# Seven block products for four row tiles of dW_q, and another order of the column and m transposes, in a backward kernel on one core

## The chip, the core and the metric

The kernel runs on one core of a Trainium2 chip. The metric is the device time of one execution in microseconds (us); the time of a kernel is the median of several runs. A core has TensorE (PE: matmuls, and PEld: the loads of their stationary operand), VectorE (DVE), ScalarE (ACT), GpSimd (POOL) and SyncE (SP). Here SP does no arithmetic: it issues the transposing DMAs and some plain ones, in order. POOL issues most plain DMAs. Matmuls write to PSUM, from which VectorE and ScalarE read.

## The reference

A linear-attention block and a SwiGLU feed-forward block, each behind a layer norm with a residual, and all gradients of that. S = 2048 tokens, D = 640, 32 heads of 20, F = 1728, bf16.

```python
def _A_ref(x, wqkv, wo):
    qkv = (x @ wqkv).reshape(B, S, 3, H, Dh)...
    phi = lambda t: jnp.where(t > 0, t + 1, jnp.exp(t)) + 1e-6
    pq, pk = phi(q), phi(k)
    kv = jnp.einsum("bhsd,bhse->bhde", pk, v)
    z = jnp.einsum("bhsd->bhd", pk)
    num = jnp.einsum("bhqd,bhde->bhqe", pq, kv)
    den = jnp.einsum("bhqd,bhd->bhq", pq, z)[..., None] + 1e-6
    return (num / den)... @ wo
def _B_ref(x, w_gate, w_up, w_down):
    return (silu(x @ w_gate) * (x @ w_up)) @ w_down
h = x + _A_ref(_layernorm(x), A_wqkv, A_wo)
h2 = h + _B_ref(_layernorm(h), B_w_gate, B_w_up, B_w_down)
# outputs: h2, and the gradients to x, wqkv, wo, w_gate, w_up, w_down for a given grad_out
```

The change is about three pieces of it: the gradient dW_q = xn^T dq (640x640, a sum over 2048 tokens; xn the normalized x, dq the gradient at the query projection); the products that need transposed copies of two 640x640 matrices, GT and Y, for the gradients of wo and the value projection; and the last product of the forward pass, h2 = h + m W_down, which needs m (2048x1728) with its hidden index on the partitions.

## The kernel before

The kernel is one program of stages, each in lines below one another: the forward attention (lines 199 to 613), the gate and up projections with their gradients (622 to 897), the gradient through the feed-forward input and the second layer norm together with dp and dq (932 to 1212), and the last stage (1214 to 1599), which the change touches. Tokens are tiled in 16 tiles of 128 (ST = 16), D in 5 tiles of 128 (DT = 5), and outputs 640 wide are computed in two halves of 320 columns, so that one PSUM buffer (two banks; the pool has four buffers) holds a tile of 128x640. In a block `tc.manual_schedule(engines=...)` the named engines issue in the order of the program; the other engines are ordered by a planner that may let a later instruction go first.

The part of the program around the change, in its order:

- Lines 1170 to 1212, the end of the dp/dq stage. `dp_mm(t)` (987) makes dp of token tile t on TensorE and evicts it on ScalarE (993); `dp_1(t, ts)` (1170) does VectorE's first part (997 to 1000), widens two vectors on ScalarE (1005) and, for the tiles in `ts`, normalizes xn on ScalarE (`xn_act`, 1021); `dp_2` (1176) finishes dq on VectorE. `gt_part` (926) accumulates GT = dh1^T pqs beside it.
- Lines 1214 to 1302, a block in which SP and VectorE keep the order of the program. SP issues the 16 transposes of wqkv (1231 to 1237), the rest of GT runs on TensorE, `ps_dz` follows (1257 to 1262), and `load_pk` (1222), `load_pqT` (1275), `wk2` (1279) and `dwqk_steps` (1285) are defined. `dwqk(0, i)` is row tile i of dW_q: 2 halves x 16 token tiles = 32 matmuls of 128x320, an eviction on ScalarE (1295) and a store from POOL (1296).
- Lines 1304 to 1322: `dwqk(0, 0)`, the masked blocks `kv_blocks` (534, 540 and 543) that need all of GT, `dwqk(0, 1)`, `wk2(0..4)` mixed with `dwqk(0, 2)`, and the broadcast `ps_dzb`. Each `wk2(i)` is 7 small matmuls, an eviction and a transpose on SP (1283).
- Lines 1338 to 1390, the dk loop, with steps t = 0 to 18. Step t makes dk of token tile t (10 matmuls at 1353, VectorE at 1350, 1354 and 1356, a transpose on SP at 1357), and, for token tile u = t - 3, dxn (30 matmuls at 1382, three products of which the last needs the transposed dk) and the layer norm's backward pass (`ln_bwd`, 143). SP also issues two transposes for tile u + 3 in each step (`load_pqT`). Steps 2 and 3 begin with `dwqk(0, 3)` and `dwqk(0, 4)`. Steps 8 to 13 transpose the six column blocks of GT (`tr_cols`, 1361). Step 14 transposes KV. Step 16 loads w_down (1369, 1371). From u = 11 on (`MTA = 5`) each step transposes one m tile (`load_mT`, 1330), which is 128 tokens x 1792. From step 16 on, `dwqk(1, i)` does row tiles of dW_k.
- Lines 1509 to 1599, the last part, with TensorE, ScalarE and POOL in the order of the program. It computes m W_down for two token tiles at a time by seven block products (`step_a` to `step_f`, p = 0 to 6; `osum` makes the block sums of m on VectorE, 1430) and the last two tiles directly (`tail`, 1571). Before it SP transposes m tiles 5 and 6 and Y columns 0 and 1, then in step p = 0, 1, ... m tiles 2p+7 and 2p+8 and Y columns 2p+2 and 2p+3. Small products (`dwo`, `dwv`) go between the steps from a queue, `small_q`; the last two `dwv` stand after the first half of tile 14 and before `step_d(6)`.

The m tiles live in four tiles of a pool with four buffers that also holds dq, the transposed ring and wvk; so each group of four m tiles can only be loaded when one of these has been read for the last time. `mats` is one 17x640 region of SBUF in which GT, woT, dKVT, KV, G, Y and a sum in fp32 follow one another.

Of the kernel before, what the change touches and what calls it, by code (L numbers as in the profile page):

```python
# [8 lines left out]
FP32 = mybir.dt.float32  # L9
# [6 lines left out]
P = 128  # L16
# [4 lines left out]
def kernel(  # L21
# [23 lines left out]
    GM = 448  # L45
    MTA = 5
    HKG = 13
# [884 lines left out]
    with tc.manual_schedule(engines={EngineType.PE, EngineType.DVE, EngineType.Activation, EngineType.SP, EngineType.Pool}):  # L932
# [237 lines left out]
        def dp_1(t, ts=()):  # L1170
            dp_a(t, prs[t % 2])
            widen(rxs[t % 2], rall, t)
            xn_act(ts)
            widen(prs[t % 2], nS1, t)
# [5 lines left out]

        dp_1(ST - 5)
        dp_mm(ST - 4)
        dp_1(ST - 4)
        dp_2(ST - 5)
# [3 lines left out]
        dp_mm(ST - 3)  # L1188
        dp_1(ST - 3, range(6, 8))
        dp_2(ST - 4)  # L1190
# [22 lines left out]

    with tc.manual_schedule(engines={EngineType.SP, EngineType.DVE}):

# [6 lines left out]
        def load_pk(t):  # L1222
            pkrs[t] = small.tile([P, D], BF16, name="pkr", tag="stg", bufs=3, padded_shape=[P, 7 * P])
            pool_store(pkrs[t][:], scr_pk_v[:, t, :])

        load_pk(0)
        load_pk(1)
        def tr_cols(dst, src, c):
            nc.sync.dma_start_transpose(out=dst.unsqueeze(1), in_=src[:, c:c + P])
# [80 lines left out]
        nc.vector.tensor_tensor(out=half(zacc), in0=row(ps_dz), in1=half(dmask[:]), op=ALU.mult)  # L1310
        dwqk(0, 0)
        kv_blocks(dKVT, "ps_dkvt", lambda i, a, b: woT[:, i, a:b], lambda i, a, b: GT[:, i, a:b])
        dzs = [wk("dzs"), wk("dzl")]
        nc.vector.tensor_copy(out=dzs[0][:], in_=zacc)
        nc.vector.tensor_tensor(out=dzs[1][:], in0=zacc, in1=dzs[0][:], op=ALU.subtract)
        dwqk(0, 1)
        for i in range(3):
            wk2(i)
        dwqk(0, 2, lambda: [wk2(i) for i in range(3, DT)])
        ps = mm("ps_dzb")  # L1320
        mm_row(ps, lambda k: ones[:], lambda k, n0, n1: dzs[k][:, n0:n1], 2)
        nc.scalar.copy(out=half(dzb[:]), in_=row(ps))

        dk = big.tile([P, ST, D], BF16, name="dk", tag="B")
        mTs = {}
# [12 lines left out]
        for t in range(ST + LAG):  # L1338
            if t >= ST:
                for i in ((0,), (1, 2), (3,))[t - ST]:  # L1340
                    load_h1(i)
            if t in (2, 3):
                dwqk(0, t + 1)
            if t < ST:
                if t + 2 < ST:
                    load_pk(t + 2)
                if t in (2, 6):
# [8 lines left out]
                nc.vector.tensor_tensor(out=dk[:, t, :], in0=tk[:], in1=pkr[:], op=ALU.mult)  # L1356
                nc.sync.dma_start_transpose(out=ring[:, t % 4], in_=dk[:, t, :])
                if t < 2:
                    load_pqT(t + 1)
            if 8 <= t < 8 + HG:  # L1360
                tr_cols(G[:, t - 8, :], scr_GT, OH[t - 8])
            if t == 14:
# [21 lines left out]
            if u + 3 < ST:  # L1384
                load_pqT(u + 3)
            if ST - MTA <= u:
                load_mT(u - ST + MTA)
            dx = wk("dx")
# [120 lines left out]
        with tc.manual_schedule(engines={EngineType.PE, EngineType.Activation, EngineType.Pool}):  # L1509
            for t in (4, 5):  # L1510
                load_h1(t)
            for t in (5, 6):
                load_mT(t)
            for j in range(2):
                tr_cols(Y[:, j, :], scr_Yt, OH[j])
            tt(T1, B12, B11)
# [14 lines left out]
            for p in range(NP):  # L1531
                v = p - 1
                for t in (2 * p + 4, 2 * p + 5):
                    if p > 0 and t < ST:
                        load_h1(t)
                for t in (2 * p + 7, 2 * p + 8):
                    if t < ST:
                        load_mT(t)
                for j in range(2 * p + 2, min(2 * p + 4, HG)):
                    tr_cols(Y[:, j, :], scr_Yt, OH[j])  # L1540
                step_a(p)
# [36 lines left out]
            tail(ST - 2, 0, 320, p14[:, 0, :320])  # L1578
            for f, i in small_q:
                f(i)  # L1580
            step_d(v)
            tail(ST - 2, 320, D, p14[:, 1, :320])
            c22(v)
# [46 lines left out]
```

## Time and profile before

| | us |
|---|---|
| median of 3 runs | 791.06 (788.67 to 811.74) |
| the profiled execution's own time | 790.5 |
| its span, first to last instruction | 788.8 |
| mean granted TensorE clock | 0.996 of full speed |

Read the profile so: the busy time of an engine is the sum of its instructions; TensorE's matmuls are pipelined, so the duration of one (about 299 ns for 128x320) is longer than the distance between two starts. "Waits" give, for an engine and a line, how long the engine stood idle before it, and which instruction released it. The chain of waits is followed back from the last instruction. The DMA share is the mean busy share of 16 DMA engines; packets that wait in a queue count, so it can be above 1. The stages in time: the dp/dq stage ends near 586, dW_q and wk2 run from 586 to 617 with the first four dk tiles, the dk loop from 617 to 711, and the last product from 711 to 786.

### The profile page before, as it was taken

Reading aid. Unit: us, or ns where it says so; the run is one execution under the profiler, and the core shown is the slowest. Engines: PE = TensorE matmul, PEld = TensorE weight load, DVE = VectorE, ACT = ScalarE, POOL = GpSimd, SP = SyncE. Lnnn points to the kernel's source line nnn. Section 1 sums busy time; section 2 is a strip of 40 time slices with the busy share of each in tenths; the row PEclk is TensorE's granted clock in tenths of the full one; section 3 lists DMA queues with packets and bytes.
Section 4 is the critical chain, followed back from the end, with each engine's and each line's share of the span. In section 5 each row is a group of like instructions: output and inputs, shape, how many; then the busy total and the mean of one; then the engine's idle time right before and its main releaser. Section 6 shows DMA issues by size and latency. Waiting matters only on the chain.

```text
span 788.8 us, 13752 instructions
## 1 busy us (share of the span) xinstructions
PE 778.6 (99%) x5243; PEld 500.3 (63%) x5243; DVE 575.9 (73%) x1005; ACT 331.6 (42%) x490; POOL 224.8 (28%) x380
## 2 busy tenths in 40 slices
PE   9999999999999999999999999999999999999988
PEld 7676566555555555555666677777767777777756
DVE  7979988894788548848888668999862466627753
ACT  6962532670184036501841245667652233323001
POOL 4600037513301120145231444341421122123310
PEclk9999999999999999999999999999999999999989
DMA  9799999999979997999899899999899888999992
GB/s 263 162 243 307 200 220 280 264 246 227 227 178 224 203 214 179 238 256 225 208 230 161 282 268 187 211 241 221 182 249 176 160 187 174 170 253 222 211 222 77
DMA packets 295012, 170.54 MB, mean 216 GB/s; under 512 B 242765, under 2 KB 282702, under 8 KB 294945
## 3 DMA queue, kind: packets, MB, share of 16 engines
q1 hardware_dynamic: 271472, 102.75, 66.0%
q0 software_dynamic: 20032, 63.34, 29.0%
q10 hardware_dynamic: 3440, 3.56, 1.4%
q8 instruction: 41, 0.67, 0.4%
q14 instruction: 27, 0.21, 0.1%
HBM read 52.84 MB, written 56.28 MB: 138 GB/s over the span
## 4 chain that ended last, share of the span: by engine, by line
PE 91%; DVE 3%; DMA 2%; SPq 2%; issue 1%; ACT 1%; POOL 0%; ACTq 0%; DVEq 0%
PE ps_dw L881 10%; PE ps_dxn L1382 8%; PE ps_wa L690 7%; PE pg L796 7%; PE pu L801 7%; PE ps_dhn L955 7%; PE ps_dwqk L1290 6%; PE ps_dm L423 5%; PE ps_dhc L955 5%; PE ps_kq L311 4%; PE ps_wc L690 3%; PE ps_dk L110 3%; PE ps_y L514 3%; PE ps_a L577 3%; PE ps_oa L1446 2%; PE pdm L423 2%
## 5 line engine op out<-in xcount | busy, mean ns | idle before, releaser
L955 PEld LDWEIGHTS <-cols 128*128 128x128 bf16 x624 | 61.0, 98 | 23.8
L796 PE MATMUL pg<-wgu,hnT 128*128 128x448 bf16 (+1 forms) x320 | 63.6, 346 | 0.0
L801 PE MATMUL pu<-wgu,hnT 128*128 128x448 bf16 (+1 forms) x320 | 63.6, 346 | 0.0
L881 PE MATMUL ps_dw<-m_s,dh 128*128 128x448 bf16 (+1 forms) x320 | 60.4, 346 | 0.0
L1382 PEld LDWEIGHTS <-ring 128*128 128x128 bf16 x480 | 47.0, 98 | 18.2
L1382 PE MATMUL ps_dxn<-wqkvT,ring 128*128 128x320 bf16 x320 | 51.3, 299 | 0.0
L801 PEld LDWEIGHTS <-hnT 128*128 128x128 bf16 x320 | 31.3, 98 | 27.1
L881 PEld LDWEIGHTS <-dh 128*128 128x128 bf16 x320 | 31.3, 98 | 27.1
L796 PEld LDWEIGHTS <-hnT 128*128 128x128 bf16 x320 | 31.3, 98 | 27.0
L423 PEld LDWEIGHTS <-dh2T 128*128 128x128 bf16 x320 | 31.0, 98 | 25.1
L423 PE MATMUL ps_dm<-wdT,dh2T 128*128 128x448 bf16 (+1 forms) x240 | 46.5, 344 | 0.0
L817 ACT ACTIVATE dd<-pg 128x896 bf16<-128x896 f32 (+1 forms) x32 | 28.5, 890 | 40.4 <-PE pg L796 40.4
L311 PE MATMUL ps_kq<-wqk,xnT 128*128 128x320 bf16 x320 | 44.9, 299 | 0.6 <-DMA xnT<-xn 0.5
L311 PEld LDWEIGHTS <-xnT 128*128 128x128 bf16 x320 | 30.8, 98 | 13.0 <-DMA xnT<-xn 0.9
L690 PEld LDWEIGHTS <-S 128*128 128x128 bf16 x256 | 25.0, 98 | 21.7
L1290 PEld LDWEIGHTS <-hn 128*128 128x128 bf16 x320 | 31.0, 98 | 12.1 <-issue 0.3
L140 POOL TENSOR_SCALAR lnv<-mv 128x1 f32<-128x1 f32 x32 | 11.9, 373 | 89.8 <-DVE mv L136 73.8
L843 POOL DMA_DIRECT2D scr_m<-m_s x16 | 12.1, 757 | 88.0 <-DVE m_s L829 88.0
L148 DVE CUSTOM_DVE_ANT_0 lb_a<-lb_dy,hn 128x640 bf16<-128x640 bf16 x16 | 13.2, 826 | 30.2 <-ACT lb_dy L146 29.3
L686 DVE TENSOR_TENSOR dd<-dd 128x3584 bf16<-128x3584 bf16 (+1 forms) x12 | 23.1, 1954 | 13.4 <-PE ps_wa L690 13.4
L146 ACT ACTIVATE lb_dy<-ps_dxn,rstd 128x640 bf16<-128x640 f32 x16 | 12.7, 793 | 45.1 <-PE ps_dxn L1382 45.1
L977 POOL DMA_DIRECT2D dh<-lb_a x16 | 14.6, 910 | 58.1 <-DVE lb_a L976 57.7
(261 smaller groups left out, 1797.5 us busy)
## 6 DMA issues: line engine op xcount, KB each, us to landing
scr_dT<-stg SPq DMA_DIRECT2D x48, 224.0 KB, 3.2
cols<-scr_dT POOLq DMA_DIRECT2D x21, 448.0 KB, 6.1
scr_m<-m_s POOLq DMA_DIRECT2D x12, 448.0 KB, 4.8
pq<-scr_pq POOLq DMA_DIRECT2D x32, 160.0 KB, 5.8
hn<-in_A_x_dram SPq DMA_DIRECT2D x5, 640.0 KB, 5.7
scr_dT<-stg SPq DMA_DIRECT2D x16, 192.0 KB, 2.3
cols<-scr_dT POOLq DMA_DIRECT2D x7, 384.0 KB, 5.6
scr_pq<-pqa SPq DMA_DIRECT2D x4, 640.0 KB, 4.5
```

The lines of the kernel that those rows point to most:

```text
L110: nc.tensor.matmul(ps[:, ci, :320], lhsT=lhs(k), rhs=rhs(k, *NCH[ci]), start=(start and k == 0), stop=(stop and k == n - 1))
L311: nc.tensor.matmul(ps[:, ci, :320], lhsT=xnT[:, t, k, :], rhs=wqk[:, k, w0 + n0:w0 + n1], start=(k == 0), stop=(k == DT - 1))
L423: nc.tensor.matmul(ps[:, c, :w], lhsT=dh2T[:, kt, (t + c) * P:(t + c + 1) * P], rhs=wdT[:, kt, o:o + w], start=(kt == 0), stop=(kt == DT - 1))
L514: nc.tensor.matmul(ps[:, ci, :320], lhsT=xn[:, t, i * P:(i + 1) * P], rhs=pk[:, t, n0:n1], start=(t == 0), stop=(t == ST - 1))
L690: nc.tensor.matmul(out, lhsT=lhs[:, t, :], rhs=rhs[:, t, :], start=(first and t == 0), stop=(t == 7), skip_group_check=not first)
L796: nc.tensor.matmul(pg[:, c, :w], lhsT=hnT[:, kt, (t + c) * P:(t + c + 1) * P], rhs=wg[:, kt, 0:w], start=(kt == 0), stop=(kt == DT - 1))
L801: nc.tensor.matmul(pu[:, c, :w], lhsT=hnT[:, kt, (t + c) * P:(t + c + 1) * P], rhs=wg[:, kt, w:2 * w], start=(kt == 0), stop=(kt == DT - 1))
L817: sig = nc.scalar.activation(out=dg, in_=pg[:, :, :w], func=ACT.Sigmoid)
L881: nc.tensor.matmul(ps[:, c, :w], lhsT=lhs(t), rhs=rhs(t), start=(t == 0), stop=(t == ST - 1))
L955: nc.tensor.matmul(out, lhsT=lhs[:, k, :], rhs=rhs[:, k, :], start=(first and k == 0), stop=(k == HKG - 1), skip_group_check=not first)
L1290: nc.tensor.matmul(ps[:, ci, :320], lhsT=xn_r[:, t, i * P:(i + 1) * P], rhs=dq[t // 8][:, t % 8, n0:n1] if which == 0 else dk[:, t, n0:n1] ...
L1382: nc.tensor.matmul(ps[:, ci, :320], lhsT=lhs[:, i, :], rhs=rhs[:, i, n0:n1], start=(k == 0 and i == 0), stop=(k == 2 and i == DT - 1))
```

## The change

Four parts, all in the last two stages:

1. Row tiles 0 to 3 of dW_q are computed as a 2x2 block problem: rows in two halves of two row tiles each (m = 0, 1, with u = 0, 1 inside), tokens in two halves of 8 tiles (k = 0, 1), columns in two halves of 320 (n = 0, 1). Seven products of 8 matmuls for each u replace eight. The sums of blocks that they need (T of dq, 8x320 per partition; S of xn, 8x128) are made on VectorE, and so are the combinations; ScalarE copies partial results from PSUM to SBUF. Three of the four PSUM buffers are held by the products meanwhile. Row tile 4 keeps its 32 matmuls and stands in the middle, and the `wk2` are between the products. The last product of u = 0 and 1 (`p3q`) is done in steps 0 and 1 of the dk loop, and its combinations (`c12q`) in step 1. `kv_blocks` moves ahead of all of them. TensorE and ScalarE now keep the order of the program in this block and so through the dk loop.
2. GT's columns are transposed in steps 3 to 8 of the dk loop, Y's in steps 8 to 13; the third pkr tile is loaded ahead, and the others by the end of a step instead of the beginning of the next.
3. The m tiles start at u = 10: tile 0 to 2 in u = 10 to 12, two each in 13 and 14, one in 15 (`MT_AT`). The last part then transposes m tiles 2p+8 and 2p+9 in step p, with no Y columns between.
4. Two passes of `xn_act` move to the two `dp_1` before, one each, and the last `dwv` moves behind `step_d(6)`.

```diff
@@ -43,7 +43,7 @@
     NKT = 27
     FT = 14
     GM = 448
-    MTA = 5
+    MT_AT = (10, 11, 12, 13, 13, 14, 14, 15)
     HKG = 13
     assert (S, D, F) == (2048, 640, 1728)
 
@@ -1178,15 +1178,15 @@
             load_q(t + 3)
             return last
 
-        dp_1(ST - 5)
+        dp_1(ST - 5, range(6, 7))
         dp_mm(ST - 4)
-        dp_1(ST - 4)
+        dp_1(ST - 4, range(7, 8))
         dp_2(ST - 5)
         for i in (0, 1):
             gts[i] = mm("ps_gt")
             gt_part(gts[i], i, 0, ST - 4, ST if i else 4)
         dp_mm(ST - 3)
-        dp_1(ST - 3, range(6, 8))
+        dp_1(ST - 3)
         dp_2(ST - 4)
         nc.gpsimd.dma_start(out=hn[:, ST - 4:ST, :], in_=x_v[:, ST - 4:ST, :])
         store_dwd(p - 1)
@@ -1211,7 +1211,7 @@
         xn_act(range(9, ST - 4))
         last_dq = dp_2(ST - 1)
 
-    with tc.manual_schedule(engines={EngineType.SP, EngineType.DVE}):
+    with tc.manual_schedule(engines={EngineType.SP, EngineType.DVE, EngineType.PE, EngineType.Activation}):
 
         wqkvT = big.tile([P, 16, D], BF16, name="wqkvT", tag="B")
         xn_r = hn
@@ -1225,6 +1225,7 @@
 
         load_pk(0)
         load_pk(1)
+        load_pk(2)
         def tr_cols(dst, src, c):
             nc.sync.dma_start_transpose(out=dst.unsqueeze(1), in_=src[:, c:c + P])
 
@@ -1308,20 +1309,98 @@
                                         scalar2=rstd1[:, t:t + 1], op0=ALU.subtract, op1=ALU.mult)
         zacc = mats[:, 15 * D:17 * D].bitcast(FP32)
         nc.vector.tensor_tensor(out=half(zacc), in0=row(ps_dz), in1=half(dmask[:]), op=ALU.mult)
-        dwqk(0, 0)
         kv_blocks(dKVT, "ps_dkvt", lambda i, a, b: woT[:, i, a:b], lambda i, a, b: GT[:, i, a:b])
+
+        dk = big.tile([P, ST, D], BF16, name="dk", tag="B")
+        dkf = dk.rearrange("p t d -> p (t d)")
+        U2 = (0, 1)
+        NB = 8 * 320
+        Ta = dkf[:, 16 * D - NB - 16 * P:16 * D - 16 * P].rearrange("p (k n) -> p k n", k=8)
+        S3q = [dkf[:, 16 * D - 8 * P * (2 - u):16 * D - 8 * P * (1 - u)].rearrange("p (k c) -> p k c", c=P) for u in U2]
+        Tb = mat(2 * HG * P, 8, 320)
+        Sq = [mat(2 * HG * P + NB + 8 * P * u, 8, P) for u in U2]
+
+        def xb(m, k, u):
+            return xn_r[:, 8 * k:8 * k + 8, (2 * m + u) * P:(2 * m + u + 1) * P]
+
+        def db(k, n):
+            return dq[k][:, :, 320 * n:320 * n + 320]
+
+        def vv(out, in0, in1, op=ALU.subtract):
+            nc.vector.tensor_tensor(out=out, in0=in0, in1=in1, op=op)
+
+        def kept():
+            return wk("kept", pool=1)[:].bitcast(FP32)
+
+        def prod8(out, lhs, rhs, start=True):
+            for k in range(8):
+                nc.tensor.matmul(out, lhsT=lhs[:, k, :], rhs=rhs[:, k, :], start=(start and k == 0), stop=(k == 7),
+                                 skip_group_check=not start)
+
+        pq_a = [mm("ps_dwa") for _ in U2]
+        Aq = [p[:, 0, :320] for p in pq_a]
+        Dq = [p[:, 1, :320] for p in pq_a]
+        for u in U2:
+            prod8(Aq[u], xb(0, 0, u), db(0, 0))
+        s1q = [kept() for _ in U2]
+        for u in U2:
+            nc.scalar.copy(out=s1q[u], in_=Aq[u])
+        vv(Ta, db(0, 1), db(0, 0))
+        for u in U2:
+            prod8(Dq[u], xb(0, 1, u), db(1, 0))
+            vv(Sq[u], xb(1, 0, u), xb(1, 1, u), ALU.add)
+        pq_c = mm("ps_dwc")
+        for u in U2:
+            prod8(pq_c[:, u, :320], Sq[u], Ta)
         dzs = [wk("dzs"), wk("dzl")]
         nc.vector.tensor_copy(out=dzs[0][:], in_=zacc)
         nc.vector.tensor_tensor(out=dzs[1][:], in0=zacc, in1=dzs[0][:], op=ALU.subtract)
-        dwqk(0, 1)
-        for i in range(3):
-            wk2(i)
-        dwqk(0, 2, lambda: [wk2(i) for i in range(3, DT)])
+        ev0, ev1 = ([wk("dwq") for _ in U2] for _ in U2)
+        for u in U2:
+            vv(ev0[u][:, 0:320], Dq[u], s1q[u], ALU.add)
+        dwqk(0, 4)
+        vv(Tb, db(1, 1), Ta)
+        for u in U2:
+            vv(Sq[u], Sq[u], xb(0, 0, u))
+        for u in U2:
+            vv(S3q[u], xb(0, 0, u), xb(1, 0, u))
+        vv(Ta, db(1, 1), db(0, 1))
+        u2q = [kept() for _ in U2]
+        for u in U2:
+            prod8(Aq[u], Sq[u], Tb, False)
+            nc.scalar.copy(out=u2q[u], in_=Aq[u])
+            wk2(u)
+        vv(Tb, db(1, 0), Tb)
+        for u in U2:
+            vv(Sq[u], xb(0, 1, u), Sq[u])
+        for u in U2:
+            prod8(Aq[u], S3q[u], Ta, False)
+            nc.scalar.copy(out=s1q[u], in_=Aq[u])
+            wk2(2 + u)
+        for u in U2:
+            vv(ev1[u][:, 320:D], pq_c[:, u, :320], s1q[u], ALU.add)
+
+        def dwq_store(i, ev):
+            nc.gpsimd.dma_start(out=out_2[i * P:(i + 1) * P, 0:D], in_=ev[:])
+
+        for u in U2:
+            prod8(Aq[u], xb(1, 1, u), Tb, False)
+            nc.scalar.copy(out=ev1[u][:, 0:320], in_=Aq[u])
+            dwq_store(2 + u, ev1[u])
+            if u == 0:
+                wk2(4)
         ps = mm("ps_dzb")
         mm_row(ps, lambda k: ones[:], lambda k, n0, n1: dzs[k][:, n0:n1], 2)
         nc.scalar.copy(out=half(dzb[:]), in_=row(ps))
 
-        dk = big.tile([P, ST, D], BF16, name="dk", tag="B")
+        def p3q(u):
+            prod8(pq_c[:, u, :320], Sq[u], db(1, 1), False)
+
+        def c12q():
+            for u in U2:
+                vv(ev0[u][:, 320:D], pq_c[:, u, :320], u2q[u], ALU.add)
+                dwq_store(u, ev0[u])
+
         mTs = {}
 
         def load_mT(t):
@@ -1339,11 +1418,9 @@
             if t >= ST:
                 for i in ((0,), (1, 2), (3,))[t - ST]:
                     load_h1(i)
-            if t in (2, 3):
-                dwqk(0, t + 1)
+            if t < 2:
+                p3q(t)
             if t < ST:
-                if t + 2 < ST:
-                    load_pk(t + 2)
                 if t in (2, 6):
                     load_xnT(2 + t // 6)
                 pkr = pkrs.pop(t)
@@ -1355,10 +1432,16 @@
                                                in1=half(dzb[:]), op0=ALU.mult, op1=ALU.add)
                 nc.vector.tensor_tensor(out=dk[:, t, :], in0=tk[:], in1=pkr[:], op=ALU.mult)
                 nc.sync.dma_start_transpose(out=ring[:, t % 4], in_=dk[:, t, :])
+                if t + 3 < ST:
+                    load_pk(t + 3)
+                if t == 1:
+                    c12q()
                 if t < 2:
                     load_pqT(t + 1)
+            if 3 <= t < 3 + HG:
+                tr_cols(G[:, t - 3, :], scr_GT, OH[t - 3])
             if 8 <= t < 8 + HG:
-                tr_cols(G[:, t - 8, :], scr_GT, OH[t - 8])
+                tr_cols(Y[:, t - 8, :], scr_Yt, OH[t - 8])
             if t == 14:
                 nc.sync.dma_start_transpose(out=KV.rearrange("p j c -> p (j c)").unsqueeze(1), in_=scr_KVT)
             if t == ST:
@@ -1383,8 +1466,8 @@
                                          start=(k == 0 and i == 0), stop=(k == 2 and i == DT - 1))
             if u + 3 < ST:
                 load_pqT(u + 3)
-            if ST - MTA <= u:
-                load_mT(u - ST + MTA)
+            for i in [i for i, v in enumerate(MT_AT) if v == u]:
+                load_mT(i)
             dx = wk("dx")
             ln_bwd(ps, xn_r[:, u, :], rstd1[:, u:u + 1], dh1[:, u, :], dx[:], 0)
             nc.gpsimd.dma_start(out=o1_v[:, u, :], in_=dx[:])
@@ -1509,10 +1592,6 @@
         with tc.manual_schedule(engines={EngineType.PE, EngineType.Activation, EngineType.Pool}):
             for t in (4, 5):
                 load_h1(t)
-            for t in (5, 6):
-                load_mT(t)
-            for j in range(2):
-                tr_cols(Y[:, j, :], scr_Yt, OH[j])
             tt(T1, B12, B11)
             osum(0, 0)
             tt(T2, B22, T1)
@@ -1533,11 +1612,9 @@
                 for t in (2 * p + 4, 2 * p + 5):
                     if p > 0 and t < ST:
                         load_h1(t)
-                for t in (2 * p + 7, 2 * p + 8):
+                for t in (2 * p + 8, 2 * p + 9):
                     if t < ST:
                         load_mT(t)
-                for j in range(2 * p + 2, min(2 * p + 4, HG)):
-                    tr_cols(Y[:, j, :], scr_Yt, OH[j])
                 step_a(p)
                 if v < 0:
                     tt(T4, B21, T2)
@@ -1576,9 +1653,10 @@
             v = NP - 1
             p14 = mm("ps_o")
             tail(ST - 2, 0, 320, p14[:, 0, :320])
-            for f, i in small_q:
-                f(i)
+            (f, i), (f2, i2) = small_q
+            f(i)
             step_d(v)
+            f2(i2)
             tail(ST - 2, 320, D, p14[:, 1, :320])
             c22(v)
             step_e(v)
```

## The prediction

> **What bounds the kernel now.** I read the page's busy times first, then the waits of TensorE alone, then the chain that ended last from 740 us on, then the busy time by stretches. TensorE is the bound:
>
> ```profile
> span 788.8 us, 13752 instructions
> ...
> PE 778.6 (99%) x5243; PEld 500.3 (63%) x5243; DVE 575.9 (73%) x1005; ACT 331.6 (42%) x490; POOL 224.8 (28%) x380
> ```
>
> It is idle for 10.2 us in all, so an edit can win only by giving it fewer instructions, or by ending a wait of TensorE itself. These three of its waits lie where the change works (us in total, times, longest):
>
> ```profile
> PE ps_oa L1446 <- DVE h1r L1430: 3.5, 1, 3.5
> ...
> PE ps_dp L110 <- ACT dp L993: 0.8, 1, 0.8
> PE ps_dwv L129 <- ACT dwv L1405: 0.8, 1, 0.8
> ```
>
> The chain (start, duration, what) tells what is behind the 3.5 us: not VectorE, but an m tile, and before it the Y columns on SP's queue.
>
> ```profile
> 740.09 1.34 SPq L1229
> 741.43 0.04 issue
> 741.48 2.58 SPq L1229
> 744.05 0.04 issue
> 744.09 10.85 DMA mT<-scr_m
> 754.95 0.02 issue
> 754.97 0.96 DVE os L1430 x2
> 755.93 0.41 DVE h1r L1430
> 756.34 0.04 issue
> 756.38 3.36 PE ps_oa L1446 x12
> ```
>
> In program order the transposes at L1330 give that m tile as number 11. VectorE had finished at 750.09 and stood until it came. The stretches (length, then PE, PEld, DVE, ACT, POOL busy, granted clock, DMA share, GB/s) show what it cost and where room is:
>
> ```profile
> 617.00:686.00 69.00, 69.00 (x510) 49.70 (x509) 42.33 (x98) 21.65 (x36) 14.07 (x27) 1.00 0.85 168
> ...
> 711.00:752.84 41.84, 41.84 (x313) 30.18 (x312) 29.85 (x58) 6.96 (x11) 13.50 (x25) 1.00 1.18 225
> 752.84:756.38 3.54, 0.00 (x1) 0.00 (x0) 1.41 (x4) 0.69 (x1) 0.00 (x0) 0.80 1.27 218
> 756.38:759.00 2.62, 2.62 (x10) 1.43 (x10) 1.84 (x4) 0.00 (x0) 1.62 (x3) 0.50 0.94 173
> 759.00:762.00 3.00, 3.00 (x14) 1.72 (x13) 0.98 (x2) 0.00 (x0) 0.54 (x1) 0.54 1.18 240
> ```
>
> After the idle 3.54 us the granted clock is 0.50 and 0.54 until 762. From 617 to 686 TensorE never stops and the DMA engines have room; after 711 they have none.
>
> **The change part by part.** Times are on the clock of the profile before; the sum is made against its own 790.5 us (span 788.8 and 1.7 around it). The median of the runs shown, 791.06, is 0.6 above that.
>
> *Products.* Four row tiles go from 4x32 matmuls of 320 columns to 7x2x8 = 112. The chain gives the price:
>
> ```profile
> 592.09 4.35 PE ps_dwqk L1290 x32
> ```
>
> That is 0.136 us each, so 16 fewer save 2.18 us. What pays for it on VectorE:
>
> ```profile
> L686 DVE TENSOR_TENSOR dd<-dd 128x3584 bf16<-128x3584 bf16 x9 | 17.9, 2021 | 11.2 <-PE ps_wa L690 11.2
> ...
> L686 DVE TENSOR_TENSOR S<-hn 128x1024 bf16<-128x1024 bf16 x16 | 10.1, 685 | 8.2 <-DMA stg<-dd 6.6 <-DMA out_dram<-dwd 1.6
> ...
> L1430 DVE TENSOR_TENSOR ot<-ps_oa,h1r 128x320 f32<-128x320 f32 x14 | 6.9, 492 | 10.2 <-PE ps_oa L1446 5.0 <-PE ps_oa L1452 4.8
> ```
>
> Eight sums of 1024 at 0.69 are 5.5 us, four of 2560 at 1.49 (between the two rows: (2021-685)/2560 = 0.522 ns an element) are 5.9, six combinations of 320 at 0.49 are 2.9: 14.3 us, where VectorE was busy 8.3 us of the 31 between 586 and 617. ScalarE loses four evictions of 0.69 and gets eight of 320 columns at about 0.53 (the 128x320 rows of L1038), 1.5 us more.
>
> Do they come in time? The key blocks now follow ps_dz at once (586.1); the last GT copy ended at 585.73, so ps_dz covers it. VectorE is done with zacc and the four masks near 588.5, with Ta at 590.0, with the two Sq at 591.3. TensorE spends 587.6 to 592.0 on four products, then wants Sq and Ta: 1.4 us (first Sq) in hand. The kept row tile (4.35 us) covers the casts, the two combinations, Tb, Sq, S3q and the second Ta, which end at 595.1, 596.5, 597.9 and 599.4; they are wanted at 598.5, 598.5, 601.4 and 601.4. The third Tb can start when its readers end at 601.2, ends at 602.7 and is wanted at 604.3. So about 1.5 us is in hand everywhere. On ScalarE each step asks 0.53+0.69 = 1.2 us against 0.35+1.09 = 1.4 us on TensorE (7 matmuls of wk2, 8 of the product); the one bank pair left for wk2 is given back just in time. In a fixed order a late item stalls all behind it: everything up to the dk tiles queues behind such a product, and dxn behind those. The nearest case is the same scheme in the gate and up gradients (L690), where the waits of TensorE list nothing: 0. From the other side, all the hands-over late by 0.1 us and one sum late by its own 1.5 us: 2.5. I take 0, as the L690 case is nearest.
>
> *Start of the dk loop.* The two row tiles that stood between the dk tiles (8.7 us) now stand ahead, so dk 0 has less time. From the start of its matmuls to its transpose on SP took 3.07 us (602.70 to 605.77). Now: start 608.6, issue 611.7, landing 3.6 later (median of ring<-dk; 2.6 to 6.1 seen): 615.3. TensorE is there after dk 0, the late product, dk 1 to 3 (5x1.36 less 0.27) and ten matmuls of dxn 0 (1.36), at 616.5: 1.2 us in hand; a landing of 6.1 costs 1.3 us. I take 0, the median; range 0 to 1.3.
>
> *SP's queue, 617 to 686.* The columns of GT move from steps 8-13 to 3-8, those of Y from the last stage to 8-13. Y's six transposes are new there. GT's took 1.22 to 1.41 us of SP each, and in their steps TensorE kept its 5.43 us: a step with four transposes asks about 5.1 us of SP. SP starts step 3 some 3 us late (backlog of the pq and pk transposes), gains 0.4 us a step, loses 0.9 at step 8, which has five. Behind these wait the pq tiles, issued within 5 us of the dxn that frees their slot and wanted 12.2 us after it: with 4 us of landing the hand is 3 to 4 us less the backlog, never below 0 by much. At nothing; without that cover see the slower rival.
>
> *The m tiles.* They begin at row 10: eight instead of five are issued inside the loop, at 3.5 us of SP each for the first, and delay dk 15, pq 14, pq 15 and the wd load by some 3 us. Of these the nearest is wd: landed at 710.5, wanted at 715.45, so 2 us stay. From about 711.5 SP then stands at m tile 4, as before (711.4), and goes straight on: the six Y transposes between (718.46-721.95, 732.04-735.17, 740.09-744.05) took 10.6 us. So m tile 11 is issued near 733.5 instead of 744.1 and with 10.85 us to land is there near 744.4; it was wanted at 750.1. The wait goes: 3.54 us, and the slow clock behind it: 22 matmuls from 756.38 to 762.00 took 5.62 us, at 0.136 they take 2.99, so 2.63. Together 6.17. Late next would be m tile 13: two tiles at 3.5 us behind, near 751 to 752, wanted near 757. Bounds: 0 if it lands as late as before, 6.17 if not; I take 6.17, by 5.7 us in hand.
>
> *A rule against this row.* The Trainium skill, "TensorE: Matmul & The Clock Gate", Part 1, has the clock fall to half after an idle window of about 3.4 us and come back after about 3.4 us of work. By that the slow stretch would cost an estimated 1.7 us and not 2.63, and the sum would be 9.1. The row, 0.50 to 0.54 for 5.6 us, decides.
>
> *A rule against the move.* The skill's "Trainium Kernel Development and Optimization", Key Constraints, says that transfers of all queues run on the same 16 DMA engines; so moving Y takes no DMA work away. By that alone the tail would keep its wait and the sum would be 3.8. The stretches (0.85 before 686, 1.18 after 711) show that it goes where room is.
>
> *Small waits.* Two ScalarE passes over hn (1.73 us at 569.64) stood ahead of the eviction that TensorE waited for; one each now goes into earlier idle gaps of ScalarE of 1.93 and 1.77 us. Saves 0.83. The last dwv goes behind six products and two matmuls (1.09 us) that cover the eviction of 0.69: saves 0.82. Both between 0 and that. POOL's pkr loads move by part of a step, with three buffers as before; the two xnT loads behind the third pkr come 2 us later, landed by 592 for 608: nothing.
>
> Sum: 2.18 + 6.17 + 0.83 + 0.82 = 10.0. 790.5 - 10.0 = **780.5 us**.
>
> **The rivals.**
> *The m tiles stay late.* Between 720 and 730, and 741 and 750, single m tiles held SP for 6.8 and 6.1 us; if copies slow the transposes wherever they stand, tile 11 or 13 is late again. Against it: 5.7 us in hand. All of the 6.17 lost: 786.7; a part, with a wait too short for the slow clock: about 783.
> *The block or dk 0 waits.* For it: hands of 1.2 to 1.5 us and a fixed order. 2.5 + 1.3 = 3.8 lost: 784.3.
> *SP's queue becomes the bound from step 3 to 13 (slower).* 45 transposes in 11 steps of 5.43 us (59.7). At 1.27 each they take 57; at 1.72 (the two Y transposes at 718.46, 3.44 us, beside other traffic) 77.4, which is 13 us over after the hand of 4.5: 793.7. It decides from (59.7+4.5+10)/45 = 1.65 us each. Against it: GT's 1.22 to 1.41 in this very loop.
>
> **How the numbers follow.** Forecast 0.70, m tiles late 0.13, block or dk 0 late 0.09, SP's queue 0.06, and 0.02 for a gain beyond it. The low end is the forecast less 1.8, by which the fastest run shown (788.67) lies under the profiled one: 778.7. The high end, 788.0, holds the first two rivals and 1.3 more; the third is outside. Two per cent, about what a measurement of this kernel can tell from no change, is 15.8 us: below 775 there is no term (0.03), above 807 only SP's queue at more than 2 us a transpose (half of its 0.06, so 0.03), within 0.94.
>
> **What would show it.** Right: 16 matmuls fewer, and among TensorE's waits no ps_oa, ps_dp or ps_dwv; clock 1.00 through 762; steps of 5.43 us in the dk loop. Wrong: a TensorE wait on VectorE or on an eviction between 586 and 610; a first dxn that waits for ring; steps longer than 5.43 us with SP never waiting for dk; the chain again ending in mT<-scr_m.

## The result, and the profile after

The changed kernel takes 790.70 us (median of 20 runs, 787.10 to 805.34), the kernel before on the same chip 786.78 us (20 runs, 783.88 to 811.74). The ratio, from the undisturbed runs of both, is 1.0059, 95% interval 1.0036 to 1.0081: some 4.6 us slower. The forecast was 780.5 us, and its range ended at 788.0.

The profiled executions alone would mislead: 789.3 us after, 790.5 us before. The one of before lies 3.7 us above the median of its 20 runs, and it carried the wait in the last stage and the slow clock in full. More on that below.

The busy times of the page after (span 787.6 us):

```profile
PE 776.4 (99%) x5227; PEld 498.3 (63%) x5227; DVE 589.1 (75%) x1023; ACT 332.4 (42%) x494; POOL 224.9 (29%) x380
```

TensorE has the 16 matmuls fewer that were foretold. Its waits in the same execution (us in total, times, longest):

```profile
PE ps_dxn L1465 <- DMA ring<-dq: 5.6, 1, 5.6
...
PE ps_dxn L1465 <- DMA ring<-dk: 1.1, 1, 1.1
```

All three waits that the change aimed at are gone (ps_oa, ps_dp, ps_dwv). Two new ones stand in the dk loop: dxn waits for a ring tile, once dk, once dq. By stretches (length, then PE, PEld, DVE, ACT, POOL busy, granted clock, DMA share, GB/s):

```profile
614.00:648.70 34.70, 27.93 (x203) 19.31 (x201) 20.28 (x46) 9.02 (x15) 8.93 (x16) 0.99 1.10 192
648.70:655.70 7.00, 7.00 (x42) 4.54 (x43) 0.33 (x1) 0.88 (x2) 0.00 (x0) 0.79 1.05 185
...
717.00:758.00 41.00, 41.00 (x304) 29.52 (x303) 31.13 (x61) 6.96 (x11) 13.49 (x25) 1.00 1.21 209
```

The block of products (586 to 607) has no gap, nor has the last stage (the third line) up to 758, at clock 1.00. What is lost lies between 614 and 656: 34.70 - 27.93 = 6.77 us idle, then a slow clock. The chain of what ended last (start, duration, what) leads back from the first wait to VectorE, from the second to SP's queue:

```profile
614.07 0.60 DVE tk L1431
614.67 7.50 DMA ring<-dk
...
637.51 2.05 SPq L1277
...
639.61 9.04 DMA ring<-dq
...
648.70 5.65 PE ps_dxn L1465 x30
...
655.71 4.07 PE ps_dxn L1465 x30
```

The first late tile is dk 1. SP issued it as soon as VectorE had made it; what is long is its landing, 7.50 us. The second is the dq of tile 5. It stood behind other transposes in SP's queue, was issued in step 5 at 639.61, only 3.5 us before dxn wanted it (643.15; before, 634.68 and 644.00: 9.3 us ahead), and landed 9.04 us later. The 30 matmuls behind it take 5.65 us, and 4.07 a step later: 1.58 us of slow clock. Waits and clock together cost 1.12 + 5.55 + 1.58 = 8.25 us. This nearly closes the account of the two profiled executions: products -2.21, last stage -3.54 and -2.63, small waits -0.83 and -0.82 are -10.03; with the 8.25 that is -1.8, and the spans differ by -1.2.

SP's own queue after (start, duration, what it issues):

```profile
610.70 1.20 SPq L1434 DMA_TRANSPOSE ring<-dk  x1
...
614.67 1.21 SPq L1434 DMA_TRANSPOSE ring<-dk  x1
...
619.63 5.78 SPq L1434 DMA_TRANSPOSE ring<-dk  x2
...
629.47 1.22 SPq L1434 DMA_TRANSPOSE ring<-dk  x1
...
634.75 1.22 SPq L1434 DMA_TRANSPOSE ring<-dk  x1
```

and before:

```profile
605.77 1.20 SPq L1357 DMA_TRANSPOSE ring<-dk  x1
...
609.72 1.22 SPq L1357 DMA_TRANSPOSE ring<-dk  x1
...
629.24 1.27 SPq L1277 DMA_TRANSPOSE ring<-dq  x1
632.11 1.20 SPq L1357 DMA_TRANSPOSE ring<-dk  x1
...
634.68 1.27 SPq L1277 DMA_TRANSPOSE ring<-dq  x1
```

Two differences are to be seen. First, dk 0 and dk 1 were issued at 605.77 and 609.72 and would have been wanted near 618.2 and 623.6: 12.4 and 13.9 us. Now they are issued at 610.70 and 614.67 and wanted near 615.5 and 620.9: 4.8 and 6.3 us. Second, a step had three transposes (dk, pk, dq), and after the dq SP had nothing to issue for 1.6 us (630.51 to 632.11); now it has four, and from dk to dk 629.47 to 634.75 is 5.28 us of a step of 5.43. In both kernels a few transposes hold SP longer than the usual 1.2 to 1.3 us, up to 2.87 in this profile of before and up to 4.00 after; the pair at 619.63 is one of 4.00 and one of 1.69.

So the theory to be tested was: two losses that add. (1) With the products ahead, the 8.7 us of two dW_q row tiles no longer stand between the dk tiles, and a tile of the first steps that comes late stops TensorE. (2) With four transposes a step in steps 3 to 13, SP cannot work off a hold, and dq or dk comes late at a later step. The rivals: the 640 KB xnT load of step 6 as such; POOL's burst of loads and stores at the loop's start; the order of the pk and pq transposes.

### The profile page after: what moved, and what is told of

The parts are those of the page before. It is cut to its first block, busy times and chain, and to the rows that moved or that the text cites. A ratio compares the mean times of both kernels' runs of the same rounds, so it can differ in the third digit from the quotient of the medians.

```text
span 787.6 us, 13759 instructions
## 1 busy us (share of the span) xinstructions
PE 776.4 (99%) x5227; PEld 498.3 (63%) x5227; DVE 589.1 (75%) x1023; ACT 332.4 (42%) x494; POOL 224.9 (29%) x380
## 4 chain that ended last, share of the span: by engine, by line
PE 91%; DVE 3%; DMA 3%; issue 1%; SPq 1%; ACT 0%; POOL 0%; DVEq 0%; ACTq 0%
PE ps_dw L881 10%; PE pu L801 7%; PE ps_wa L690 7%; PE pg L796 7%; PE ps_dxn L1465 7%; PE ps_dhn L955 7%; PE ps_dm L423 5%; PE ps_dhc L955 5%; PE ps_kq L311 4%; PE ps_oa L1529 4%; PE ps_dwqk L1291 3%; PE ps_wc L690 3%; PE ps_y L514 3%; PE ps_a L577 3%; PE pdm L423 2%; PE ps_dp L110 2%
## 5 line engine op out<-in xcount | busy, mean ns | idle before, releaser
L955 PE MATMUL ps_dhn<-wgT,cols 128*128 128x320 bf16 x208 | 30.8, 299 | 0.0
```

The source lines that it names most:

```text
L955: nc.tensor.matmul(out, lhsT=lhs[:, k, :], rhs=rhs[:, k, :], start=(first and k == 0), stop=(k == HKG - 1), skip_group_check=not first)
```

## The experiments

"Waits" below are those of TensorE from 586 us on in the kernel's profiled execution, in us at their time.

**Undoing the transposes, and making the moves alone.** e1 puts GT's columns back to steps 8 to 13 and Y's back to the last stage; the m tiles stay as changed:

```diff
-            if 3 <= t < 3 + HG:
-                tr_cols(G[:, t - 3, :], scr_GT, OH[t - 3])
             if 8 <= t < 8 + HG:
-                tr_cols(Y[:, t - 8, :], scr_Yt, OH[t - 8])
+                tr_cols(G[:, t - 8, :], scr_GT, OH[t - 8])
...
+                for j in range(2 * p + 2, min(2 * p + 4, HG)):
+                    tr_cols(Y[:, j, :], scr_Yt, OH[j])
```

> The changed kernel with the columns of GT back in steps 8 to 13 and those of Y back in the last stage; products and m tiles as changed. Theory: the wait of dxn for ring<-dq (5.6 us and some 1.6 us of slow clock in the profile after) needs GT's columns in steps 3 to 8, which keep SP's backlog alive until the 640 KB xnT load of step 6. Then the dk loop has no wait over 1.5 us here, and the time is about 3.8 us under the kernel before (16 matmuls, 0.83, 0.82), ratio 0.995. Rival, the products alone: with the 8.7 us of TensorE work moved ahead of the dk loop the wait stays, ratio 1.005.

Measured: 789.21 us, ratio to before 0.9991 (0.9951 to 1.0032). Waits: dq 1.75 at 622.4, dk 4.66 at 628.6, Y for ps_dwv 2.7 in two. The late dq of steps 5 and after is gone, the waits of the first steps are there: loss (1) stands without loss (2). Y in the last stage behind the new m tiles makes a wait of its own. The profiled execution took 795.71 us, 6.5 us above the median of e1, so these sizes are not those of a usual run.

e2 is the kernel before with the moves of G, Y and the m tiles alone; its edit is the lines of the diff on `MT_AT`, `tr_cols` and `load_mT`.

> The kernel before with the moves of GT, Y and the m tiles alone; dW_q, the order of TensorE and the small waits as before. Theory: without the late start of the dk loop SP has no backlog at step 3, so no wait in the dk loop, and no wait for an m tile in the last stage; ratio 0.993 to 0.998, by how large that wait is in the usual run of the kernel before. Rival, the moves alone: TensorE waits for ring<-dq or ring<-pk in the dk loop, 5 us or more, ratio 1.005 or above.

Measured: 786.82 us, ratio 0.9976 (0.9946 to 1.0005). No wait for an m tile; dq 1.59 at 679.3, and the two small waits of before (0.83, 0.82). So the moves gain some 0.24% (1.9 us, and the interval reaches just over 1), not the 6.17 us of the forecast, and bring a late dq near the end of the loop.

**The 640 KB load.** e3 cuts the two xnT loads of steps 2 and 6 into eight of 160 KB:

```diff
+        def load_xnT1(v):
+            pool_store(xnT_r[:, v], scr_xnT[v])
...
-                if t in (2, 6):
-                    load_xnT(2 + t // 6)
+                if 2 <= t < 10:
+                    load_xnT1(t + 6)
```

> The changed kernel with the two 640 KB loads of xnT at steps 2 and 6 cut into eight of 160 KB, one in each of steps 2 to 9. Theory: the large load is what holds SP's transposes for about 4 us at step 6 and makes dq 5 late; in pieces the dk loop's waits fall from 6.7 us to under 2, and the time is 5 to 7 us under that of the changed kernel, ratio 0.992 to 0.998 to the kernel before. Rival: the 160 KB of each step and four transposes are too much together in any form; the waits stay and the ratio stays near 1.006.

Measured: 789.92 us, ratio 1.0034 (1.0003 to 1.0065). Waits on dq of 0.90 at 627.8, 3.08 at 636.5, 0.58 and 0.21. Cutting the load up does not remove the waits, it moves them. What the place of the load does is seen in e9, below.

**Before, once more.** e4 is the kernel before, for a second profile.

> The kernel before unchanged, for a second profile of it. Theory: the wait for m tile 11 that the forecast took away whole (3.54 us and 2.63 us of slow clock) is larger in the first profile (790.5 us) than in the usual run (median 786.8); here the time is 784 to 787 and that wait is under 2 us with no slow clock behind. Rival: the wait is as large in each run, and something else makes the usual run faster.

Measured: 791.33 us. Its longest TensorE wait:

```profile
PE ps_oa L1446 <- DVE h1r L1430: 4.9, 3, 4.1
```

The wait in the last stage is real and comes back (4.08 at the longest), but both profiled executions lie well above the median: of 116 runs of before in these comparisons 80 had a mean granted clock of 1.000, these two 0.996 and 0.998.

This profile shows something else, which the first profile of before does not. Here is its dk 1, the 640 KB load that POOL issues beside it, and, in the view of that one transpose, its landing:

```profile
611.86 1.31 SPq L1357 DMA_TRANSPOSE ring<-dk  x1
...
611.94 0.76 POOL L165 DMA_DIRECT2D xnT_r<-scr_xnT  x1
```

```profile
DMA to landing us min/median/max: 10.0/10.0/10.0
```

So dk 1 lands as late as in any changed kernel (9.99 us, at 621.85), and another dk holds SP for 5.27 us, yet the dk loop has no wait: dk 1 was wanted at 623.54, 11.7 us after its issue. With 7.6 us less lead it would have been late by 5.9 us.

**The products alone.** e5 is the changed kernel with G, Y and the m tiles in the places of before.

> The changed kernel with the columns of GT and Y and the m tiles all as before; products, fixed order, small waits and the early third pkr tile as changed. Theory: the products alone already cost most of what they save, since SP starts the dk loop late: a dxn of tile 1 to 6 waits 2 us or more for ring<-dq or ring<-dk, the fastest run is near 783 (3 us over the 780.3 that the fastest run before less 3.8 gives), ratio 0.997 to 1.002. Rival: the products cost nothing and only GT's early columns do; then no such wait, ratio 0.995 or less.

Measured: 788.94 us, ratio 1.0017 (0.9985 to 1.0049). One long wait, the transpose that it waited for, and SP behind it:

```profile
PE ps_dxn L1463 <- DMA ring<-dk: 4.0, 1, 4.0
```

```profile
617.51 10.40 DMA ring<-dk
```

```profile
623.20 7.54 SPq L1434 DMA_TRANSPOSE ring<-dk  x2
```

The late tile is dk 1 again. It was issued 3.97 us behind dk 0, as in the kernel before (3.95), and took 10.40 us to land. The next two, dk 2 and dk 3, hold SP for 4.73 and 2.71 us (7.54 with the 0.10 between), but come in time. That is loss (1) by itself: the products, which save 2.2 us of TensorE, save nothing.

**Order on SP and POOL.** Three tries to give the first dk tiles a freer queue. e6 issues pqT(1) before the loop and pqT(2) in step 0; e7 issues the third pkr load behind the two xnT loads instead of ahead; e8 does both.

```diff
 e6
+        load_pqT(1)
         ps = mm("ps_dzb")
...
-                if t < 2:
-                    load_pqT(t + 1)
+                if t == 0:
+                    load_pqT(2)
 e7
-        load_pk(2)
...
         load_xnT(0)
         load_xnT(1)
+        load_pk(2)
```

> The changed kernel with the pq and pk transposes of tile 1 issued before the dk loop, where SP stood idle for 2.6 us (608.1 to 610.7 in the profile after), and those of tile 2 in step 0. Theory: the waits come from SP's backlog at the start of the loop, which is 2.5 to 5 us smaller now and can't be worked off later at 5.28 us of SP in a step of 5.43: the waits of dxn fall from 6.7 us to under 3, the time by 3 to 6 us, ratio 0.997 to 1.001. Rival: the four transposes in each of steps 3 to 13 are too much wherever the loop starts; the waits only come later, ratio 1.004 or above.

> The changed kernel with the third pkr load behind the first two xnT loads on POOL's queue, so that these go 2.5 us earlier, as before. Theory: they then collide less with SP's transposes of wqkv, which end at 595 to 597 in place of 598.6, and SP's backlog is some 2 us smaller: ratio 1.001 to 1.004. Rival: the end of the wqkv transposes is set by the 800 KB store of GT, which does not move: end at 598 to 600 and ratio 1.006 as the changed kernel.

> The two edits together (pq and pk transposes of tile 1 ahead of the dk loop, third pkr load behind the xnT loads). Theory: backlog 4 to 6 us smaller, no wait of dxn over 1.5 us, ratio 0.993 to 0.998. Rival: as in the two before, ratio 1.004 or above.

Measured: e6 794.08 us, ratio 1.0058 (1.0014 to 1.0101), dk 2.09 at 624.8 and dq 0.35; e7 791.74 us, 1.0041 (1.0001 to 1.0082), dq and dk late five times, up to 2.97; e8 791.44 us, 1.0063 (1.0025 to 1.0102), dk 4.18 and dq 1.59. None helps, though e8's wqkvT transposes ended at 595.0 (598.5 in the changed kernel). The order of these few transfers is not the cause. In all three the late dk is dk 1. The profiled execution of e6 took 784.96 us, 9 us under its median, so its two waits do not explain that median.

**Burst apart, cover back.** e9 moves, in the program, two of POOL's stores from step 1 to steps 3 and 4 and the xnT loads from steps 2 and 6 to 5 and 9. e10 gives part of the cover back: one row tile (4.35 us) goes from the middle of the products to step 2 of the dk loop. e11 does both, and e12 does both with G, Y and the m tiles in the places of before.

```diff
 e9
-                dwq_store(u, ev0[u])
...
-                if t in (2, 6):
-                    load_xnT(2 + t // 6)
+                if t in (3, 4):
+                    dwq_store(t - 3, ev0[t - 3])
+                if t in (5, 9):
+                    load_xnT(2 + t // 9)
 e10
-        dwqk(0, 4)
         vv(Tb, db(1, 1), Ta)
...
             if t < 2:
                 p3q(t)
+            if t == 2:
+                dwqk(0, 4)
```

> The changed kernel with the copies that POOL issues at steps 1 to 3 spread: the two last dW_q stores at steps 3 and 4, the xnT loads at steps 5 and 9 in place of 2 and 6. Theory A: the 2 to 4.7 us for which SP stands at the dk transposes of steps 1 to 3 come from this burst (1.1 MB in 4 us); without it dk 1 to 3 are issued in under 1.5 us each, the first waits of dxn fall from 1.1 to 4.2 us to under 1, ratio 0.998 to 1.002. Theory B: dk 0 to 2 and pq 1 and 2 simply have too little lead; holds of 2 us remain from the pkr loads and the waits stay, ratio 1.004 or above.

> The changed kernel with the kept row tile of dW_q (32 matmuls, 4.35 us) moved from the middle of the products to step 2 of the dk loop, so that the first dxn comes that much later after its dk. It loses the cover of VectorE's sums: some 2 us of waits of ps_dwa for VectorE between 593 and 600. Theory B: the lead decides; the waits of dxn for ring in the first six steps vanish or fall under 1 us, slow clock with them, ratio 0.997 to 1.002 in spite of the 2 us. Theory A (the burst) and the rival of too many transposes: waits for ring stay, ratio 1.006 or above.

> Both edits, copies spread and row tile 4 in step 2. Theories A and B together: no wait of dxn over 0.5 us in the loop, only the 2 us of ps_dwa; ratio 0.994 to 0.999. If waits for ring-<dq come in steps 6 to 13 all the same, the four transposes of each step are the remaining cause, ratio 1.002 or above.

> As the one before, but GT's and Y's columns and the m tiles as in the kernel before. If the four transposes in steps 3 to 13 cost something still: less than the one before by 1 us or more. If the moves help once the lead is there (as the moves alone did, 0.9976): more than the one before by 1 to 2 us, with a wait for an m tile in the last stage. Ratio 0.995 to 1.000.

On the chip the stores did not move. POOL is not among the engines that keep the order of the program here, and it issues both 3.2 us behind dk 0 (618.41 in e9), as in the changed kernel (613.87 and 610.70):

```profile
621.57 1.08 POOL L1384 DMA_DIRECT2D out_dram<-dwq  x2
```

The stores of e11 and e12 too go out within 4 us of dk 0. So e9 tests the place of the xnT loads alone.

Measured: e9 790.68 us, 1.0045 (1.0015 to 1.0075): no wait in the first steps, and dk 1 lands after 4.34 us; then dq 1.97 at 645.7, 1.92 at 671.2, 0.81 at 688.5. e10 787.87 us, 0.9990 (0.9958 to 1.0023): none in the first steps either, then

```profile
PE ps_dxn L1466 <- DMA ring<-dq: 5.1, 2, 3.1
```

The row tile was also what covered VectorE in the block: without it two hands-over are late, 0.69 and 0.27 us. e11 787.85 us, 1.0015 (0.9993 to 1.0037): dq 3.08 and 0.52. e12 786.13 us, 0.9985 (0.9951 to 1.0020): no wait in the dk loop, 0.63 and 0.27 in the block, 1.33 for an m tile. So loss (1) is gone with one row tile between the dk tiles, and loss (2) with the places of before, in which steps 3 to 7 have three transposes.

e12 changed three things at once; e13 leaves the loads as in the changed kernel and keeps the cover and the old places.

> The changed kernel with the row tile of 4.35 us moved from the middle of the block products to step 2 of the dk loop (as e10) and with G, Y and the m tiles in the places of before; POOL's burst of stores and loads stays as changed. It is the missing cell between e5 (old places, no cover: dk 4.02 us late), e10 (cover, new places: dq 2.00 and 3.07 us late) and e12 (cover, old places, burst apart: no wait). Theory that there are two causes which add, the lost cover at the loop's start and the four transposes a step in steps 3 to 13: no TensorE wait above 0.7 us in the dk loop, the ps_oa wait of the last stage present, ratio to before 0.996 to 1.000. Rival, that the burst is a third cause of its own: a wait of 1 to 4 us on dk or dq in steps 1 to 7, ratio 1.001 to 1.005.

Measured: 784.73 us beside 789.22 for before in the same comparison, ratio 0.9953 (0.9912 to 0.9994). It is the one version whose interval lies below 1. As evidence of a gain that is weak: it is one of thirteen ratios, it just clears 1, and before was slower in this comparison than in the others (medians of 785.51 to 787.80). No wait for an m tile came, though one was expected. The longest of its waits, and its SP queue in the first steps:

```profile
PE ps_dwa L1337 <- DVE mats L1330: 0.6, 1, 0.6
```

```profile
622.27 4.07 SPq L1278 DMA_TRANSPOSE ring<-dq  x1
626.45 1.22 SPq L1435 DMA_TRANSPOSE ring<-dk  x1
...
631.00 1.20 SPq L1435 DMA_TRANSPOSE ring<-dk  x1
```

The holds are all there, one of 4.07 us on a single dq. They cost nothing: the next step takes SP 4.55 us from dk to dk instead of 5.43, its dq is off the queue at 630.30, and SP is idle until 631.00. With lead and with room on SP the loads of steps 2 and 6 cost no wait. Put in a square:

| | four transposes in steps 3 to 13 | places of before |
|---|---|---|
| no row tile in the loop | changed kernel: 1.0059; dk 1.12, dq 5.55 | e5: 1.0017; dk 4.02 |
| one row tile in step 2 | e10: 0.9990; dq 2.00, 3.07 | e13: 0.9953; none |

Each step to the right or down gains 0.4 to 0.7% by the medians of these ratios; single neighbours' intervals overlap, so the sizes are rough, while which tile is late in which cell is read from one profile each. The pattern holds over all fifteen profiles. Of the eight with the products and no row tile in the loop, seven have a wait of 0.90 us or more before 632 us (all but e9); of the other seven none has one. All nine with the new places of GT's and Y's columns have a dq late after 640 us, by 0.35 to 5.55 us at their longest; none of the six with the old places has one.

**What makes dk 1 late.** In every version in which a dk is late it is dk 1. Read from the same fifteen profiles, its time to landing goes with the load of step 2; in the changed kernel POOL issues that load 0.27 us behind dk 1 (614.67):

```profile
614.94 0.76 POOL L165 DMA_DIRECT2D xnT_r<-scr_xnT  x1
```

| dk 1 is issued | in | dk 1 to landing, us |
|---|---|---|
| within 0.6 us of the 640 KB load of step 2 | changed, e1, e4, e5, e6, e7, e8 | 7.50, 12.97, 9.99, 10.40, 8.38, 11.08, 10.51 |
| 0.3 us ahead of a 160 KB piece | e3 | 6.21 |
| 1.1 to 2.3 us ahead of the 640 KB load | before, e2, e10, e13 | 2.61, 5.71, 3.91, 4.31 |
| with that load moved to step 5 | e9, e11, e12 | 4.34, 4.16, 4.33 |

So, as far as these profiles show, loss (1) takes two things: a landing of 7.5 us or more beside that load, and a lead of 6 us in place of 12 to 14. Before has the first (e4) without the second. e9 removes the first alone, and its first steps have no wait, though its time is no better (1.0045). e10 and e13 give lead back; the row tile also puts the load further behind dk 1, which there lands early. But dk 2 takes 8.78 and 10.61 us in them and is in time by 1.5 and 0.7 us: without the 4.35 us of the row tile it would have been late. Why a transpose beside such a load lands late was not tested.

## Why the prediction was wrong

**Right, with sizes.** *Products*: forecast 2.18. In the chain of the changed kernel 25.86 us pass from the start of the block (585.74) to the end of dk 1 (611.60), five row tiles included; before, the same work takes from 586.21 to 614.28 (the end of its dwqk row 3 at 609.93, and 4.35 for the next): 28.07, so 2.21 saved. *Hands in the block*: 0 taken, 0 found; where the row tile left the block (e10 to e13) 0.9 to 1.0 us came, inside the bound of 2.5. *Small waits*: 0.83 and 0.82, both gone. *The m tiles*: the wait for tile 11 is gone in the profile after and in e2, e10 and e11. *dk 0*: forecast to be issued at 611.7; it was at 610.70 and was not waited for.

**Failed: "Start of the dk loop".** The step priced dk 0 alone, at the median landing, and ended with "a landing of 6.1 costs 1.3 us". The tile that came late was dk 1, by 1.12 us in the changed kernel and by 4.02 in e5. SP had not delayed it (3.97 us behind dk 0, as before); it took 7.50 and 10.40 us to land. The change took 7.6 us of lead from each of these tiles and left dk 1 with 6.3. The step should have priced that lead for each of them, and against the 640 KB load that now starts 0.27 us behind dk 1 and not 2.3. The landings in the profile before, up to 6.9 us, would alone have given 0.6 us; that the kernel before also has landings of 9.99 us, and covers them, is seen in e4. e10 against the changed kernel, and e13 against e5, show the lead's part: with one row tile of 4.35 us there the first waits are gone.

**Failed: "At nothing" for SP's queue.** The step said that a step of four transposes "asks about 5.1 us" and "gains 0.4 us a step". It asks 5.28 and gains 0.15, so a backlog of 3 us needs 20 steps and not eight. The dq of tile 5, which before is issued 9.3 us ahead of its use, has 3.5 us left, less than the median dq landing of 4.1. From 637 to 646 three holds follow one another (2.05, 2.84, 3.31), and the second of them, the dq of step 5, lands after 9.04 us. With three transposes a step the same queue gains some 1.6 us a step; in e13 a hold of 4.07 us was made good in the step behind it. The rival that SP's queue becomes the bound named the right queue and side, at a chance of 0.06, but with a condition that never came true: its 1.65 us a transpose on average. From 619 to 686 the 45 transposes held SP 65.5 us, 1.46 each (1.32 before). What decides is not the mean but single late tiles in a queue with no room. Why single transposes are held was not separated. They come most often behind the 640 KB loads, and where e9 moves these the holds move with them (2.44 us at 3.4 us behind the first, 2.71 at 5.5 behind the second); but some stand far from any, as 2.87 us at 670.49 in before.

**Mis-sized: the 6.17 us of the last stage.** The sum was made against an execution of 790.5 us, and the median of before over 20 runs is 786.78. A wait of 3.54 us with a slow clock behind it is not what most runs of before pay: 80 of 116 keep a mean clock of 1.000. The moves alone (e2) gained 0.24%, 1.9 us, net of a late dq of 1.59 us in its profile. That the median run's wait is shorter is argued from the clock, not shown, since no profile of such a run exists. Nor is that move always needed: e13 has the old places and no wait there, e5 and e12 have 1.07 and 1.33.

**The slow clock on the other side.** Of the changed kernel's 20 runs two have a mean clock of 1.000, of e13's twelve eight. The forecast gave a price for the clock only where it was to be won back. Behind the wait of 5.55 us the clock was:

```profile
648.70:652.00 3.30, 3.30 (x14) 1.89 (x15) 0.00 (x0) 0.00 (x0) 0.00 (x0) 0.56 1.12 166
```

The prediction set the rule of the Trainium skill ("TensorE: Matmul & The Clock Gate", Part 1) aside for the row of before, 2.63 us. Here, 1.58 us were lost, near the 1.7 estimated from that rule; the row of before was one case, not the price.

## What to carry to other kernels

When work is moved out from between the producers of a queue, price the lead that every tile in that queue loses, not that of the first tile, and set it against the longest holds and landings that the trace shows, in more than one profile if there is one. Look also at which large load now starts beside those tiles. A queue that is in order needs idle time in each step: ask how many steps it takes to work off the longest single hold, since a mean per transfer that still fits says nothing on that. Before a wait is taken as a gain, look whether the profiled execution is a typical run.

## What the runs showed of the hardware

A DMA transpose that takes SP 1.2 to 1.3 us at the median held it for up to 2.87 us in the dk loop of before (5.27 in its second profile, e4), 4.00 in the changed kernel and 4.07 in e13. A ring tile there landed after 2.6 us at the least; at the most after 6.9 us in before (10.9 in e4), 10.2 in the changed kernel and 10.6 in e13. The holds and the late landings gather behind the 640 KB loads: in the fourteen profiles that have these whole (all but e3), from 608 to 686 us, 40 of the 112 transposes issued within 8 us behind one held SP for 2 us or more, and 32 of the other 579. The ring tiles among them landed after 6.9 us at the median, the others after 3.8. No edit removed all holds.

The clock's fall does not follow the length of the wait alone. It fell to 0.59 and 0.51 in the 3.4 to 3.5 us after waits of 3.07 and 3.08 us (e10, e11), but also after 1.97 us in e9 and 2.24 us in e7:

```profile
646.00:650.00 4.00, 4.00 (x21) 2.40 (x19) 1.91 (x4) 0.00 (x0) 1.09 (x2) 0.61 1.13 209
```

```profile
627.80:632.00 4.20, 4.18 (x31) 3.04 (x32) 0.29 (x1) 0.89 (x2) 0.00 (x0) 1.00 1.06 228
...
686.00:690.00 4.00, 3.94 (x20) 2.52 (x21) 1.96 (x5) 0.00 (x0) 0.55 (x1) 0.68 1.02 198
```

The first line is e9 after its 1.97 us. The other two are e7: no fall after 2.97 us at 627.8, a fall after 2.24 us at 686. The page of the Trainium skill named above ("TensorE: Matmul & The Clock Gate", Part 1) speaks of an idle window of about 3.4 us; a shorter wait is no safe one here, and what else it depends on was not tried.
